# One load queue in order of need, pre-scaled down weights for the last block, a last output tile in two halves, and new order priorities in a transformer block on one core

## The chip, the cores and the metric

The kernel runs on one core of one Trainium2 chip. The metric is the device time of one execution in microseconds (us). "Span" is the time from the first to the last instruction in a profile; the timed figure is about 1.8 us longer (span 222.2, time 224.05 for the profiled run of the kernel before).

Each run carries the mean clock that was granted to the matmul engine: 1.0 is full speed. A run is called slow when it takes over 1.5% more than the fastest of the same kernel. Comparisons below are between fast runs, unless a sentence says otherwise.

## The reference

A transformer block on x of 2048 tokens by 448 features, in bf16. A condition vector c of 448 numbers gives six vectors of 448.

```python
mod = (silu(c) @ w_mod).reshape(1, 6, 1, 448)
sa, ca, ga, sb, cb, gb = [mod[:, i] for i in range(6)]
h = layernorm(x) * (1 + ca) + sa
x = x + ga * attention(h, wqkv, wo)   # 16 heads of 28; each token sees 8 tokens, at distances 0, 2, ..., 14
h = layernorm(x) * (1 + cb) + sb
gate, up = h @ W_gate, h @ W_up       # 448 -> 1792
x = x + gb * ((gate * (gate > 0) * up) @ W_down)
```

## The kernel before

The kernel is a list of operations. Each has an engine, a cost in ns, a priority, and what it reads and writes. At build time a greedy scheduler (`_Plan`) takes these and fixes, once and for all, the order of instructions on each engine: PE (matmuls), ScalarE (ACT), VectorE (DVE), GpSimd (POOL) and SP (which issues loads). On the chip nothing is reordered; an engine whose next instruction isn't ready waits.

The two numbers SWITCH and XLAT and the table of priorities steer the scheduler. The kernel computes the same whatever they are.

```python
PR = {
    "ln1": [537, 334, 2613, 2241],
    "qk": [711, 1230, 2349, 2507],
    # ... cut: ten more rows like these
    "misc": [2507, 2310, 2251, 237],
}
class _Plan:
    SWITCH = 105.0      # expected cost of a change of PE tiling shape
    XLAT = 95.0         # expected latency from one engine to another
    # ...
    # in schedule(): among the ready operations of an engine, the smallest priority number goes first
                sel = min((c for c in cl if c[0] <= tmin + slack[e]), key=lambda c: (c[1], c[2]))
```

Loads are put on SP's queue, except for two on ACT's:

```python
        load_x(0, 2, -9, eng=ACTE)                                        # x tiles 0 and 1, 224 KB
        load(crow[:], c..., ["crow"], 4096, -9, eng=ACTE)                 # c, 0.9 KB in 112 rows
        for i, (k0, k1) in enumerate(PARTS_A):
            load(wmod[0:112, k0:k1, 0:2 * D], ...)                        # first modulation's weights
            if i == 0:
                load_x(2, 4, -8)
        # ... cut: Wv, Wqk, x 4-8, the attention gate's weights, x 8-12, wo
        load_x(12, 16, -4)
        load(wmod[0:112, :, 3 * D:6 * D], ..., ["wmodB0", "wmodB1"], ...) # second modulation's weights, 1176 KB
        # ... cut: Wgate, Wup, Wdown
```

The head of the kernel needs two things before it can transform the first tokens: silu(c), by exp on ACT, then add, reciprocal and multiply on DVE, then the modulation matmuls on PE; and the layer-norm statistics of the tokens, by `bn_stats` on DVE. When both are there, PE transposes the normalized tokens and ACT and DVE write them back as `hT` with scale and shift. Then come the first matmuls of size, the value projection.

The output stage and the last down projection:

```python
        def stage_out(t, buf, eng, eprio):
            o = _Buf(o_slots)
            op(DVE, 620, ... tensor_tensor(o.at, buf.at[:, 0:D], gbc[:, 1, :], ALU.mult) ...)   # times gb, from PSUM
            op(eng, 400 if eng == DVE else 1030, ... tensor_tensor(o.at, o.at, x_sb[:, t, :], ALU.add) ...)
            op(SP, 0, ... dma_start(out2d[128 * t:128 * t + 128, :], o.at) ...)

        def stage_down1(b, hh, prio, eprio):       # blocks 0 and 3; blocks 1 and 2 use 64-row pairs
            for j in range(4):
                # ... 14 matmuls of 128x448 into buf
                stage_out(4 * b + j, buf, DVE if b == NB - 1 else POOL, eprio)
```

The softmax here doesn't subtract the row's maximum and nothing guards it: scores larger than these inputs give would overflow.

## Time and profile before

| | before |
|---|---|
| time, median of 3 runs | 224.74 us (224.7 to 225.2) |
| span, granted clock | 222.2 us, 1.000 |
| PE busy | 212.7 us (96%) |
| first value matmul | 11.58 us |
| last down stage (56 matmuls) starts | 207.09 us |

These are lines of the page of the kernel before: busy time by engine, the busy share in 40 equal slices in tenths (5.6 us each), and the granted clock.

```profile
PE 212.7 (96%) x2452; PEld 102.7 (46%) x2452; DVE 143.3 (65%) x299; ACT 119.5 (54%) x210; POOL 49.1 (22%) x73
...
PE   7699999989999999999999999999999999999992
...
DVE  2889999888879967842387659569444304544251
ACT  2658799989879697340286676822333301433200
...
PEclk9999999999999999999999999999999999999999
...
PE 87%; DVE 4%; ACT 3%; DMA 3%; issue 1%
```

PE is the bottleneck: it is 87% of the chain that ended last (the bottom line). It isn't the bottleneck everywhere. In the first two slices it is not full, and from slice 4 to 13 DVE and ACT are each busy 70% or more, so that a delay of theirs can become a wait of PE's. The clock is full throughout.

PE's waits between 10 and 75 us, in the kernel before (columns: engine, output and line that waited, what it waited for: us in total, times, longest):

```profile
PE psF L832 <- DVE qT L818: 0.5, 1, 0.5
PE psF L619 <- DVE hb L556: 0.5, 1, 0.5
PE psF L619 <- DVE hT L696: 0.4, 1, 0.4
PE psF L681 <- ACT kT L703: 0.2, 1, 0.2
```

These are few: between 11.58 and 72 us PE is busy for 58.59 of 60.42 us.

The head, in the timeline of the kernel before. Columns: start, duration, engine, source line, operation, output<-input, count; in brackets the idle time before it and what ended that.

```profile
0.77 0.45 ACTq L446 DMA_DIRECT2D x_sb<-in_A_x_dram  x1
1.25 0.49 ACTq L446 DMA_DIRECT2D crow<-in_c_dram  x1
...
5.49 0.63 DVE L538 BATCH_NORM_STATS2 st<-x_sb 128x6 f32<-128x448 bf16 x1 [2.80 <-DMA x_sb<-in_A_x_dram]
...
6.93 0.21 ACT L490 ACTIVATE cexp<-crow 112x4 f32<-112x4 bf16 x1 [4.91 <-DMA crow<-in_c_dram]
...
7.85 0.55 PE L507 MATMUL psF<-silu,bigR 112*128 112x1 bf16 x16 [1.71 <-DVE silu L493]
```

DVE waits for the first activations until 5.49, ACT for c until 6.93. The chain of waits shows the later of the two, as "1.25 5.66 DMA crow<-in_c_dram".

The tail, in the timeline of the kernel before:

```profile
207.09 10.77 PE L930 MATMUL psF<-Wd,bigR 128*128 128x448 bf16 x56
...
217.89 0.62 DVE L891 TENSOR_TENSOR o_sb<-psF,gbc 128x448 bf16<-128x448 f32 x1 [1.53 <-PE psF L930]
218.55 0.39 DVE L893 TENSOR_TENSOR o_sb<-o_sb,x_sb 128x448 bf16<-128x448 bf16 x1
```

After the last matmul come a multiply from PSUM and an add, about 1.1 us, before the last store can be issued. All of it is on the critical path.

### The profile page before, as it was taken

The numbers are of one execution on the slowest core, as the hardware profiler recorded it, in microseconds if no ns is written. First come the engines' busy times: TensorE is split into PE (matmuls) and PEld (weight loads), VectorE is DVE, ScalarE is ACT, GpSimd is POOL, SyncE is SP. The second block draws the span as 40 slices with busy tenths as digits, with TensorE's granted clock in tenths as the row PEclk, the third lists the DMA queues.
The fourth block names the chain that finished last, engine by engine and source line by source line (L and its number), as shares of the span: only waits on it lengthen the run. The fifth ranks groups of instructions, "written<-read, shape, count | busy, mean of one in ns | idle before, by whom it ended". The sixth has DMA issues, their size and how long they took to land.

```text
span 222.2 us, 5740 instructions
## 1 busy us (share of the span) xinstructions
PE 212.7 (96%) x2452; PEld 102.7 (46%) x2452; DVE 143.3 (65%) x299; ACT 119.5 (54%) x210; POOL 49.1 (22%) x73
## 2 busy tenths in 40 slices
PE   7699999989999999999999999999999999999992
PEld 3344345555534445445544455554444454444450
DVE  2889999888879967842387659569444304544251
ACT  2658799989879697340286676822333301433200
POOL 7402450310220020028302001281660005100000
PEclk9999999999999999999999999999999999999999
DMA  6999999900130030021302000240440001100011
GB/s 174 334 274 237 200 229 238 274 5 3 27 71 3 0 52 3 0 52 41 103 24 47 3 3 1 50 96 31 91 109 21 3 0 41 44 0 3 1 41 43
DMA packets 19634, 16.52 MB, mean 74 GB/s; under 512 B 9624, under 2 KB 17880, under 8 KB 19608
## 3 DMA queue, kind: packets, MB, share of 16 engines
q1 hardware_dynamic: 19208, 15.92, 29.6%
q8 instruction: 19, 0.31, 0.6%
q10 hardware_dynamic: 400, 0.23, 0.4%
q14 instruction: 7, 0.06, 0.1%
HBM read 10.84 MB, written 1.84 MB: 57 GB/s over the span
## 4 chain that ended last, share of the span: by engine, by line
PE 87%; DVE 4%; ACT 3%; DMA 3%; issue 1%
PE psF L875 29%; PE psF L681 10%; PE psF L930 10%; PE psF L912 10%; PE psF L877 9%; PE psF L724 6%; PE psF L832 6%; PE psL L763 3%; DMA crow<-in_c_dram 3%; PE psF L796 2%; PE psF L808 1%; PE psF L619 1%; ACT EA L776 1%; DVE qT L696 1%; DVE EA L782 1%
## 5 line engine op out<-in xcount | busy, mean ns | idle before, releaser
L877 PE MATMUL psF<-h2T,Wgu 64*128 64x512 bf16 x392 | 87.7, 376 | 0.0
L875 PE MATMUL psF<-h2T,Wgu 64*128 64x512 bf16 x392 | 87.7, 376 | 0.0
L883 ACT ACTIVATE g_sb<-psF 128x512 bf16<-128x512 f32 x56 | 33.4, 597 | 52.8 <-PE psF L877 52.5
L885 DVE TENSOR_TENSOR bigR<-psF,g_sb 128x512 bf16<-128x512 f32 x56 | 38.6, 690 | 30.4 <-ACT g_sb L883 30.2
L875 PEld LDWEIGHTS psF<-h2T,Wgu 64*128 64x128 bf16 x392 | 36.2, 94 | 33.8 <-DVE st L538 0.2
L877 PEld LDWEIGHTS psF<-h2T,Wgu 64*128 64x128 bf16 x392 | 36.2, 94 | 9.8
L776 ACT ACTIVATE EA<-psL 128x912 bf16<-128x912 f32 (+1 forms) x36 | 33.3, 925 | 12.6 <-PE psL L763 12.5
L556 POOL TENSOR_SCALAR hb<-x_sb,rstd,nmr 128x448 bf16<-128x448 bf16 x22 | 15.5, 716 | 87.2 <-DVE nmr L549 81.5
L681 PE MATMUL psF<-hT,Wqk 64*128 64x512 bf16 x224 | 27.9, 377 | 0.5 <-ACT kT L703 0.2
L782 DVE TENSOR_TENSOR EA<-EA,maskA 128x912 bf16<-128x912 bf16 (+1 forms) x36 | 23.1, 646 | 6.6 <-ACT EA L776 6.1
L891 DVE TENSOR_TENSOR o_sb<-psF,gbc 128x448 bf16<-128x448 f32 x16 | 9.7, 622 | 22.7 <-PE psF L930 13.2
L912 PE MATMUL psF<-Wd,bigR 64*128 64x448 bf16 x224 | 22.5, 349 | 0.0
L538 DVE BATCH_NORM_STATS2 st<-x_sb 128x6 f32<-128x448 bf16 x32 | 19.7, 614 | 3.1 <-DMA x_sb<-in_A_x_dram 2.8
L930 PE MATMUL psF<-Wd,bigR 128*128 128x448 bf16 x112 | 21.5, 353 | 0.0
L893 POOL TENSOR_TENSOR o_sb<-o_sb,x_sb 128x448 bf16<-128x448 bf16 x12 | 12.2, 1031 | 26.3 <-DVE o_sb L891 26.3
L681 PEld LDWEIGHTS psF<-hT,Wqk 64*128 64x128 bf16 x224 | 9.6, 94 | 13.3 <-PE psF L681 2.8
L930 PEld LDWEIGHTS psF<-Wd,bigR 128*128 128x128 bf16 x112 | 10.8, 98 | 10.4 <-issue 0.4
L912 PEld LDWEIGHTS psF<-Wd,bigR 64*128 64x128 bf16 x224 | 10.8, 94 | 9.9
L832 PE MATMUL psF<-wo_pad,qT 64*128 64x448 bf16 x128 | 14.6, 350 | 0.6 <-DVE qT L818 0.5
L724 PE MATMUL psF<-Wv,hT 64*128 64x448 bf16 x126 | 14.2, 352 | 0.3
L572 POOL TENSOR_SCALAR h2T<-h2T,modc 128x512 bf16<-128x512 bf16 (+1 forms) x14 | 11.0, 797 | 13.4 <-DMA h2T<-hb 13.4
L818 DVE TENSOR_TENSOR qT<-psF,lnD 128x456 bf16<-128x456 f32 (+1 forms) x18 | 11.3, 627 | 2.2 <-ACT lnD L816 2.1
(75 smaller groups left out, 212.9 us busy)
## 6 DMA issues: line engine op xcount, KB each, us to landing
out_dram<-o_sb SPq DMA_DIRECT2D x16, 112.0 KB, 1.7
Wd<-in_B_W_down_dram SPq DMA_DIRECT2D x1, 1568.0 KB, 26.5
x_sb<-in_A_x_dram SPq DMA_DIRECT2D x3, 448.0 KB, 9.3
Wgu<-in_B_W_gate_dram SPq DMA_DIRECT2D x3, 448.0 KB, 17.5
Wgu<-in_B_W_up_dram SPq DMA_DIRECT2D x3, 448.0 KB, 19.5
bigR<-in_w_mod_dram SPq DMA_DIRECT2D x1, 1176.0 KB, 15.5
bigR<-in_w_mod_dram SPq DMA_DIRECT2D x2, 392.0 KB, 6.7
h2T<-h2T SPq DMA_DIRECT2D x3, 256.0 KB, 3.1
```

Source lines behind the costliest of these rows:

```text
L538: op(DVE, 613, lambda e: e.bn_stats(stt[:, t, :], x_sb[:, t, :]), r=[("x", t)] + list(extra), w=[(tag, "st", t)], prio=prio)
L681: last = e.matmul(bufs[sec].at, Wqk[h0:h0 + 64, k, c0:c0 + 128], hT[h0:h0 + 64, k, KOFF + TB * b:KOFF + TB * b + TB], start=(phase == 0 an ...
L724: last = e.matmul(bufs[i].at[0:nk, 0:D], hT[h0:h0 + 64, k, KOFF + k0:KOFF + k0 + nk], Wv[h0:h0 + 64, k, :], start=(phase == 0 and n == 0), ...
L776: return e.activation(dst, src, ACT.Exp)
L782: return e.tensor_tensor(d, d, msk[0:nk, None, 0:nq].to_broadcast([nk, 8, nq]), ALU.mult)
L832: last = e.matmul(bufs[i].at[:, 0:D], qT[h0:h0 + 64, g, s0:s0 + 128], wo_pad[h0:h0 + 64, g, :], start=(phase == 0 and g == 0), stop=(phase ...
L875: e.matmul(bufs[0].at, Wgu[0:64, c, 128 * f:128 * f + 128], h2.at[0:64, kg, :], start=(c == 0), stop=(c == 6))
L877: last = e.matmul(bufs[1].at, Wgu[64:128, c, 128 * f:128 * f + 128], h2.at[64:128, ku, :], start=(c == 0), stop=(c == 6))
L883: op(ACTE, _act(TB), lambda e, gs=gs, gb=bufs[0]: e.activation(gs.at, gb.at, ACT.Relu), r=[bufs[0]], w=[gs], prio=eprio)
L885: op(DVE, _dve(TB), lambda e, gs=gs, ub=bufs[1], f=f: e.tensor_tensor(hh.at[:, f, :], ub.at, gs.at, ALU.mult), r=[bufs[1], gs] + ([hh] if ...
L912: last = e.matmul(bufs[i].at[:, 0:D], hh.at[rows[i], f, 128 * (j + i):128 * (j + i) + 128], Wd[rows[i], f, :], start=(phase == 0 and f == ...
L930: last = e.matmul(buf.at[:, 0:D], hh.at[:, f, 128 * j:128 * j + 128], Wd[:, f, :], start=(f == 0), stop=(f == NF - 1))
```

## The change

The intent, part by part:

1. **Queue.** c goes first and alone on ACT's queue; the first activations go first on SP's queue, ahead of the modulation weights. All large loads are then in one queue, in the order in which they are needed.
2. **Tail.** Under the last gate/up stage GpSimd multiplies the down weights by gb once (14 multiplies). The last block then needs one add from PSUM instead of a multiply and an add, and its last tile is computed and added in two halves of 224 columns, so that the final add is shorter.
3. **Order.** A new table of priorities and new cost parameters for the scheduler: another order on every engine.

```diff
 PR = {
-    "ln1": [537, 334, 2613, 2241],
-    "qk": [711, 1230, 2349, 2507],
+    "ln1": [1460, 60, 2830, 2572],
+    "qk": [191, 2415, 509, 2324],
     # ... cut: every other row of the table changes likewise
 }
-    SWITCH = 105.0
-    XLAT = 95.0
+    SWITCH = 95.0
+    XLAT = 80.0
+    OVERLAP = {PE: 0.0, ACTE: 85.0, DVE: 75.0, POOL: 40.0, SP: 0.0}
 # ... cut: the scheduler lets an operation start OVERLAP ns before the end of the one ahead on its engine;
 # ... cut: three cost estimates (_mm, PE_DRAIN, transposes) are lowered
-        load_x(0, 2, -9, eng=ACTE)
         load(crow[:], c.rearrange("o (p k) -> (o p) k", k=4), ["crow"], 4096, -9, eng=ACTE)
+        load_x(0, 2, -9)
 # ... in stage_down1
-                stage_out(t, buf, DVE if b == NB - 1 else POOL, eprio)
+                scaled = b == NB - 1
+                cols = ((0, D // 2), (D // 2, D)) if scaled and j == 3 else ((0, D),)
+                for n, (n0, n1) in enumerate(cols):
+                    # ... the 14 matmuls, on columns n0 to n1
+                    if scaled:
+                        op(DVE, _dve(n1 - n0), ... tensor_tensor(
+                            o.at[:, n0:n1], buf.at[:, 0:n1 - n0], x_sb[:, t, n0:n1], ALU.add) ...)
+                # ... then one store of the tile
 # ... in the loop over blocks, before the last gate/up stage
+            if b == NB - 1:
+                for f in range(NF):
+                    op(POOL, 1030, lambda e, f=f: e.tensor_tensor(Wd[:, f, :], Wd[:, f, :], gbc[:, 1, :], ALU.mult),
+                       r=[("Wd", f), ("gbc", 1)], w=[("Wd", f)], prio=3000, port=True)
```

## The prediction

> **What bounds it now.** The tensor engine (PE). The page shows PE busy 96% at full clock, and the chain of waits is 87% PE. Busy time hides stalls, so I took starts from the timeline: a gate/up group of 14 matmuls starts 1.51 us before the next, the last 56 down matmuls take 10.7 us. From the first real matmul (11.58 us) to the last (217.9) are 206.3 us; summing matmuls at those undisturbed pitches leaves about 190. The other 16 us, by my count: 66 changes of tiling shape at about 0.11 us (7 us), two modulation groups (1 us), and 5 to 6 us of real waits, nearly all before 72 us, where the timeline shows gaps and the windows show VectorE and ScalarE about 90% busy. After 72 us PE is nearly gapless. Outside PE: an 11.6 us head and a 4.3 us tail.
>
> **Removed, added, moved.**
> - Head: today the 0.9 KB load of c waits behind an activation load on its queue; issued 1.25, landed 6.91. Then exp, silu and the second layer-norm statistics run late. With c first I estimate landing near 3 us (an output store lands in 1.7 us), and the first activations earlier as they no longer share with modulation weights. The bytes do not change; the Trainium skill ("Trainium Kernel Development and Optimization", Key Constraints) says queues share the same 16 DMA engines, and the trace agrees (DMA saturated, slices 2 to 8). First value-projection matmul: 10.5 instead of 11.58, gain 1.1 us.
> - But the new order puts all 32 modulation matmuls of the second layer norm early on PE (before the first softmax-denominator matmul), and they wait for a load that lands at 27.1 us today and has as many bytes ahead of it after. By content PE arrives near 25: a stall of 1 to 2 us that gives the head's gain back. Before, these matmuls ran at 33.6.
> - Tail: one add from PSUM (0.62 us) replaces multiply (0.62) plus add (0.39), and for the last tile covers 224 columns, about 0.39. Last matmul to store shrinks from 1.08 to about 0.45; 14 more matmuls cost about 0.06. Net 0.6 us, wholly on the critical path.
> - Gating: 14 GpSimd multiplies, about 1.03 us each as in the output add (14.4 us), plus two output adds, must fit under the last gate/up stage (21.2 us). They do, with about 4 us to spare: no cost, no gain but the tail's.
> - Order: the same matmuls and 64 shape changes instead of 66 (0.2 us). The Trainium skill ("TensorEngine Tiling (Array Packing)", Key Properties) says a mode change drains PE; the trace shows 0.11 us. The new priorities can recover only part of the 5 to 6 us of waits; I guess 1 to 2 us net.
>
> **Predicted time: 222.4 us**, 8 in 10 between 220.3 and 224.2. Chances: faster by over 2% 0.10, within 2% 0.87, slower 0.03.
>
> **What would show it.** Right: c landing before 4 us; first value matmul near 10.5; a PE wait on the modulation-weight DMA near 25 to 27; PE's last stage 21.2 us and then 10.8 without a wait on GpSimd; last matmul to last store about 0.45 us; matmul content unchanged; PE gaps before 72 us summing to 4 to 5 us. Wrong: the modulation matmuls finding their weights landed, or PE waiting for GpSimd at the last down stage.
>
> **What would make it wrong.** If those weights land by 25, or VectorE and ScalarE run ahead during the stall so that later gaps vanish, the gain reaches 4 us or more. If the new order starves PE between 28 and 72 us (both helpers near saturation there), nothing is won. GpSimd multiplies slowed by VectorE traffic to over 1.3 us each would delay the last stage.

## The result, and the profile after

| | before | after |
|---|---|---|
| time, median of 4 runs | 224.78 us (224.70 to 225.20) | 222.00 us (221.39 to 226.04) |
| ratio of fast runs | | 0.9864 (95%: 0.9833 to 0.9895) |

A ratio is the mean time of one kernel's fast runs over that of the other's of the same rounds, so it isn't quite the ratio of the medians. The 1.4% is real.

Of the four runs after, three took 221.39 to 222.34 us at a clock of 0.997 to 0.999, and one, which is the profiled one, took 226.04 at 0.983: a slow run. Its profile shows how a slow run goes and is used for that. For the fast picture I use the profile of an experiment, split_load, whose order on the compute engines is the changed kernel's and which differs only in that one load is cut in two. It ran as fast (221.66 us by median) and its profiled run was fast: span 219.3 us at clock 0.999.

The head of that fast run, in the timeline of split_load:

```profile
0.74 0.47 SPq L478 DMA_DIRECT2D x_sb<-in_A_x_dram  x1
0.77 0.42 ACTq L478 DMA_DIRECT2D crow<-in_c_dram  x1
...
3.04 0.21 ACT L523 ACTIVATE cexp<-crow 112x4 f32<-112x4 bf16 x1 [1.02 <-DMA crow<-in_c_dram]
...
4.19 1.15 DVE L571 BATCH_NORM_STATS2 st<-x_sb 128x6 f32<-128x448 bf16 x2
...
6.03 0.54 PE L540 MATMUL psF<-silu,bigR 112*128 112x1 bf16 x16
```

exp of c starts at 3.04 instead of 6.93, the statistics at 4.19 instead of 5.49, the modulation matmuls at 6.03 instead of 7.85. The first value matmul starts at 10.32 instead of 11.58.

The tail of the same run:

```profile
204.77 10.80 PE L968 MATMUL psF<-Wd,bigR 128*128 128x448 bf16 x70
...
214.27 0.39 DVE L974 TENSOR_TENSOR o_sb<-psF,x_sb 128x224 bf16<-128x224 f32 x1 [0.72 <-PE psF L968]
215.61 0.39 DVE L974 TENSOR_TENSOR o_sb<-psF,x_sb 128x224 bf16<-128x224 f32 x1 [0.95 <-PE psF L968]
```

After the last matmul stands one add of 0.39 us. From the start of this stage to the end of the span are 14.53 us (219.3 minus 204.77), before 15.11 (222.2 minus 207.09): the tail is about 0.6 us shorter. GpSimd's 14 multiplies took about 14 us and ended at 199.65, 5.1 us before the stage that reads them, in this run as in the slow one.

PE's waits between 10 and 75 us, to set beside those of the kernel before. The fast run, split_load:

```profile
PE psF L757 <- ACT hT L674: 1.4, 2, 1.2
PE psF L829 <- DVE EA L815: 0.4, 1, 0.4
```

The slow run of the changed kernel:

```profile
PE psF L725 <- DVE mv L541: 2.4, 1, 2.4
PE psF L508 <- DMA bigR<-in_w_mod_dram: 0.7, 1, 0.7
PE psF L797 <- DVE EA L783: 0.4, 1, 0.4
```

In the slow run PE waits twice as long at the same place, for DVE instead of ACT, and then also for the second modulation's weights. What DVE was doing stands in its timeline, in the same slow run:

```profile
22.94 0.63 DVE L539 BATCH_NORM_STATS2 st<-x_sb 128x6 f32<-128x448 bf16 x1 [1.49 <-DMA x_sb<-in_A_x_dram]
23.49 0.98 DVE L643 TENSOR_SCALAR hT<-psF,modc 128x512 bf16<-128x512 bf16 x2
```

The statistics of tile 12 stand ahead of the `hT` write-back in DVE's order, and their load is late. PE waits for the write-back, which ends at 24.47 us (the list of waits names `mv`, a short instruction of DVE that ends at about the same time). In the slow run 15 of the load's 16 parts had landed by 20.1 us and the last at 22.9; in the fast run all 16 had by 19.8. The Trainium skill ("DMA: Bandwidth & Descriptors", Why a DMA increments its semaphore by 16 and not by 1) says that the 16 engines finish independently and that only the full count means all data has landed. This agrees: one late part of 16 held everything up by 2.8 us. Why one part is late in some runs isn't shown.

Then comes the larger loss. These are windows of the slow run, chosen 3.41 us long. Columns: window, length, busy time (and instructions) of PE, weight loads, DVE, ACT and POOL, then the granted clock, DMA share and GB/s.

```profile
21.85:25.26 3.41, 0.97 (x17) 0.52 (x16) 2.32 (x6) 2.27 (x3) 2.86 (x3) 1.00 1.05 192
25.26:28.67 3.41, 3.41 (x26) 1.20 (x22) 2.88 (x10) 1.86 (x4) 0.00 (x0) 0.50 1.05 213
28.67:32.08 3.41, 2.67 (x69) 1.73 (x68) 1.23 (x7) 1.67 (x4) 2.81 (x4) 1.00 1.05 228
32.08:35.49 3.41, 3.41 (x20) 1.23 (x21) 2.63 (x5) 2.11 (x4) 1.42 (x2) 0.50 1.01 223
```

The granted clock is half for two windows of 3.41 us, each after a window in which PE was partly idle. The Trainium skill ("TensorE: Matmul & The Clock Gate", Part 1: The HAM clock gate) says that the clock goes to 4/8 after at least one idle window of about 3.4 us, and that these windows run freely. The trace agrees in the size of the window and in the half, but not in the idleness: PE was busy for 0.97 and 2.67 us of the two windows before (more in the last section). Each such window costs up to 1.7 us, half its length, so the two cost up to 3.4. With the 1.2 us of longer waiting for `hT` (2.44 against 1.24) and the 0.74 us on the weights that is about 5.4 us as an upper bound, and the spans differ by 4.9.

### The profile page after: what moved, and what is told of

Read it like the earlier page. It is cut to its first block, busy times and chain, and to the rows that moved or that the text cites. A ratio compares the mean times of both kernels' runs of the same rounds, so it can differ in the third digit from the quotient of the medians.

```text
span 224.2 us, 5763 instructions
## 1 busy us (share of the span) xinstructions
PE 215.1 (96%) x2466; PEld 105.5 (47%) x2466; DVE 140.4 (63%) x297; ACT 115.3 (51%) x208; POOL 63.5 (28%) x88
## 4 chain that ended last, share of the span: by engine, by line
PE 85%; DMA 8%; POOL 3%; SPq 1%; DVE 1%; issue 1%; POOLq 0%
PE psF L876 35%; PE psF L936 10%; PE psF L913 9%; PE psF L682 9%; DMA bigR<-in_w_mod_dram 8%; PE psF L833 6%; PE psL L764 4%; PE psF L725 3%; PE psF L878 3%; PE psF L797 3%; PE psF L809 2%; SPq L447 1%; POOL maskA L423 1%; PE psF L529 1%; POOL wo_pad L418 1%
## 5 line engine op out<-in xcount | busy, mean ns | idle before, releaser
L557 POOL TENSOR_SCALAR hb<-x_sb,rstd,nmr 128x448 bf16<-128x448 bf16 x23 | 16.4, 719 | 77.3 <-DVE nmr L550 59.4
L682 PE MATMUL psF<-hT,Wqk 64*128 64x512 bf16 x224 | 27.4, 384 | 0.0
L783 DVE TENSOR_TENSOR EA<-EA,maskA 128x912 bf16<-128x912 bf16 (+1 forms) x36 | 22.5, 630 | 4.3 <-ACT EA L777 4.1
L936 PE MATMUL psF<-Wd,bigR 128*128 128x448 bf16 (+1 forms) x126 | 21.6, 332 | 0.0
L539 DVE BATCH_NORM_STATS2 st<-x_sb 128x6 f32<-128x448 bf16 x32 | 18.8, 610 | 1.5 <-DMA x_sb<-in_A_x_dram 1.5
L725 PE MATMUL psF<-Wv,hT 64*128 64x448 bf16 x126 | 15.6, 378 | 2.7 <-DVE mv L541 2.4
L892 DVE TENSOR_TENSOR o_sb<-psF,gbc 128x448 bf16<-128x448 f32 x12 | 7.2, 622 | 15.9 <-PE psF L936 7.0
L936 PEld LDWEIGHTS psF<-Wd,bigR 128*128 128x128 bf16 x126 | 12.1, 98 | 9.3 <-issue 0.4
L992 POOL TENSOR_TENSOR Wd<-Wd,gbc 128x448 bf16<-128x448 bf16 x14 | 13.9, 1033 | 0.0
## 6 DMA issues: line engine op xcount, KB each, us to landing
bigR<-in_w_mod_dram SPq DMA_DIRECT2D x1, 1176.0 KB, 17.7
```

The source lines that it names most:

```text
L539: op(DVE, 613, lambda e: e.bn_stats(stt[:, t, :], x_sb[:, t, :]), r=[("x", t)] + list(extra), w=[(tag, "st", t)], prio=prio)
L682: last = e.matmul(bufs[sec].at, Wqk[h0:h0 + 64, k, c0:c0 + 128], hT[h0:h0 + 64, k, KOFF + TB * b:KOFF + TB * b + TB], start=(phase == 0 an ...
L725: last = e.matmul(bufs[i].at[0:nk, 0:D], hT[h0:h0 + 64, k, KOFF + k0:KOFF + k0 + nk], Wv[h0:h0 + 64, k, :], start=(phase == 0 and n == 0), ...
L783: return e.tensor_tensor(d, d, msk[0:nk, None, 0:nq].to_broadcast([nk, 8, nq]), ALU.mult)
L936: last = e.matmul(buf.at[:, 0:n1 - n0], hh.at[:, f, 128 * j:128 * j + 128], Wd[:, f, n0:n1], start=(f == 0), stop=(f == NF - 1))
```

## The experiments

All are on the chip, and the kernel before ran beside them (medians 224.76, 224.89 and 224.81 us in the three batches; the first batch has after_again, only_queue, only_tail and only_order, the third early_tr, c_first, dose_after and dose_queue_tail, the second the other four). The three batches ran on three different chips, so that across batches the ratios to the kernel before are the better comparison. Every result was correct.

The scheduler decides the order, so an edit to one load would reshuffle all engines. So I let the scheduler run once, kept the order of every engine, applied the edit to that order, and computed buffers and semaphores anew from it ("order kept"). Only after_again has no edit, and in only_tail and queue_tail the scheduler, with the old priorities and costs, placed the tail's new operations itself.

The expectations of the first batch took as theory that the head's gain is mostly taken back by waits (only_queue) and that most of the gain comes from the order (only_order). The rivals were that the head's gain carries through to the end, and that the order alone does nothing or loses. Both theories failed; the rivals came nearer.

### after_again: the changed kernel once more

No edit. It fixes the size of the gain and of the spread.

> The changed kernel once more, with five timed rounds, to see its spread and, if it comes so, a profile in the fast state. My theory: its spread is wider than that of the kernel before (224.7 to 225.2) because its tensor engine waits for two loads between 20 and 30 us, and a late load both adds its delay and lets the granted clock fall. Expected: median 221.5 to 222.5, spread over 0.5 us, fast ratio 0.983 to 0.990; in the profile the first value matmul at 10.3 us and a wait of the second modulation's matmuls for their weights. Rival (the state is chance and has nothing to do with the loads): slow runs would show no longer wait for a load than fast ones.

Measured: 221.68 us by median, runs 226.77 (slow, clock 0.983), 222.09, 221.50, 221.35 and 221.68; ratio 0.9858 (0.9829 to 0.9888). The gain repeats. The wider spread that was expected does not show: the fast runs span 0.7 us, those of the kernel before 1.9 us in the same batch (224.16 to 226.10). The slow run repeats too, again the first of its set and again with one of the 16 parts of a load late and two half-clock windows. In every set of an experiment the first run is also the profiled one, so whether being first or being profiled matters is open.

### only_queue: the new queue with the old order

```diff
-        load_x(0, 2, -9, eng=ACTE)
         load(crow[:], ..., eng=ACTE)
+        load_x(0, 2, -9)                # order of all engines otherwise kept as before
```

> The kernel before with its instruction order kept on every engine, and only the load of c first on its queue and the first activations first on the other. Theory (the head's gain is real, 1.1 us, but is taken back by waits for loads and by VectorE near saturation until 72 us): between 0.2 and 0.7 us faster than before. Rival (the head's gain carries through to the end, since the tensor engine is the bottleneck all along): 1.0 to 1.2 us faster.

Measured: 223.16 us (222.50 to 223.54), ratio 0.9924 (0.9897 to 0.9952): a gain of 1.6 us by medians (1.2 us between the profiled spans), more than the theory (0.2 to 0.7) and the rival (1.0 to 1.2) had said. These are lines of its timeline:

```profile
3.24 0.20 ACT L524 ACTIVATE cexp<-crow 112x4 f32<-112x4 bf16 x1 [1.22 <-DMA crow<-in_c_dram]
3.91 0.63 DVE L572 BATCH_NORM_STATS2 st<-x_sb 128x6 f32<-128x448 bf16 x1 [1.22 <-DMA x_sb<-in_A_x_dram]
...
10.06 3.30 PE L758 MATMUL psF<-Wv,hT 64*128 64x448 bf16 x28
```

The first value matmul comes 1.52 us earlier than before (11.58), and the last down stage 1.20 us earlier (205.89 against 207.09). So most of the head's gain lasts to the end. The later loads also come earlier in this profile: tiles 12 to 15 at 19.3 us instead of 20.4 and the second modulation's weights at 25.6 instead of 27.1. That need not be the queue's doing: over the seven profiled runs with this stream of loads uncut, the weights land anywhere from 24.8 to 29.6 us.

### only_tail: the pre-scaled weights and the split tile with the old order and queue

```diff
+            if b == NB - 1:
+                for f in range(NF):
+                    op(POOL, 1030, ... Wd[:, f, :] *= gbc[:, 1, :] ...)
 # ... and stage_down1 as in the change; priorities, costs and loads as before
```

> The kernel before with its order kept, and only the pre-gated down weights and the split last tile. Theory (all of it is on the critical path): 0.6 us faster, 0.4 to 0.7; last matmul to the last store's issue falls from 1.1 to about 0.5 us; the last down stage does not wait for GpSimd. Rival (the gating slows something, or the split costs array time): no gain or a loss.

Measured: 224.40 us by median; the five fast runs lie between 224.09 and 224.47; ratio 0.9977 (0.9951 to 1.0002). That is 0.4 us by medians, with an interval that touches zero. Its profiled run took 316.15 us at a clock of 0.661. No other run did anything like it, and I have no explanation, so I use no profile of this kernel.

### only_order: the new order with the old queue and the old tail

```diff
 # ... the changed kernel with the old stage_down1 and no pre-scaled weights; order kept, then
+        x0 = T[("x", 0)]                # the load of x tiles 0 and 1
+        order[SP].remove(x0)
+        order[ACTE].insert(0, x0)       # back to ACT's queue, ahead of c
```

> The changed kernel's new order on every engine, with the old two load queues and the old last stage. Theory (most of the gain of 3 us comes from the order, by fewer waits before 72 us): 1.5 to 2.5 us faster than before. Rival (the gain comes from the head and the tail, and the order alone does nothing or loses by its early modulation matmuls): between 0.5 us faster and 1 us slower.

Measured: 226.13 us (224.97 to 226.67), ratio 1.0051 (1.0022 to 1.0079), clock 0.990 to 0.992 in five of six runs: the new order alone is a loss. Its timeline shows why:

```profile
7.33 0.17 DVE L526 TENSOR_SCALAR cexp<-cexp 112x4 f32<-112x4 f32 x1 [4.64 <-ACT cexp L525]
...
7.83 1.15 DVE L573 BATCH_NORM_STATS2 st<-x_sb 128x6 f32<-128x448 bf16 x2
...
10.80 0.40 PE L654 MATMUL psF<-ident,hb 128*128 128x128 bf16 x4 [1.65 <-ACT hb L593]
```

The new order has DVE handle c ahead of the first statistics. With the new queue c is there first and that is right. With the old queue c lands at 7.1 us, and DVE sits idle for 4.64 us although the activations had landed at 5.6. PE then has a hole of 1.65 us. The windows of the same run by 1 us show what follows:

```profile
12.00:13.00 1.00, 0.55 (x6) 0.49 (x6) 1.00 (x6) 0.95 (x2) 0.00 (x0) 0.81 1.14 259
13.00:14.00 1.00, 1.00 (x7) 0.47 (x5) 0.15 (x2) 0.77 (x3) 0.00 (x0) 0.50 1.11 259
14.00:15.00 1.00, 1.00 (x7) 0.29 (x8) 1.00 (x5) 1.00 (x3) 0.00 (x0) 0.50 1.09 312
15.00:16.00 1.00, 0.94 (x6) 0.14 (x2) 0.23 (x2) 0.43 (x1) 0.00 (x0) 0.50 1.14 243
```

One window of half clock, of about 3.4 us. The new order fits the new queue; neither is to be judged without the other.

### queue_tail: queue and tail with the old order

```diff
 # ... the kernel before with the tail of the change, its order kept, then x tiles 0 and 1 first on SP's queue
+        order[ACTE].remove(x0)
+        order[SP].insert(0, x0)
```

> Everything of the change but the new order: the kernel before's order on every engine, the new load queue, the new last stage. If the parts of the gain simply add (queue 1.6 us, tail 0.4 to 0.5 us by the runs so far), it is 2.0 to 2.2 us faster than before, near 222.6, and the order is worth what is left to the changed kernel, about 1 us. If the order has no worth of its own, this is as fast as the changed kernel (3.1 us faster than before). It should show no slow first run from loads, as its second modulation's matmuls come 8 us later.

Measured: 222.12 us (221.87 to 222.28, four runs, clock 0.998 to 1.000), ratio 0.9863 (0.9826 to 0.9900). This is the main result: with the old order, queue and tail reach 0.9863, and the whole change 0.9858 to 0.9864. The new table of priorities adds between nothing and half a microsecond, which these runs don't separate from zero. The 222.12 us are themselves half a microsecond less than the 222.6 expected if the two parts add; why isn't shown. In its profiled run, too, one part of a load was late (tiles 12 to 15 at 21.8 us, the weights at 27.4), and PE's clock stayed 1.00: the old order needs both later, the second modulation's matmuls at 33.65 us in the kernel before, against 26.00 in the new order.

### late_mod: the second modulation's matmuls moved later in the new order

```diff
+        for oid in [T[("mm", 8, 0)], T[("mm", 8, 1)], T[("gbc", 1)] - 1]:   # 32 matmuls and the gate row
+            self.move(order, PE, oid, T[("tr", 2, 3)])                     # to before block 2's transposes
+        # ... their reads on DVE and their memset moved likewise
```

> The changed kernel with only the second modulation's 32 matmuls, its gate row's 4 and their reads moved later, to just before the third block's transposes, where their weights have long landed; the rest of the order is kept. Theory (in the changed kernel the tensor engine stands about 1 us, from 24.7 to 25.7, for these weights in a fast run): 0.5 to 1.2 us faster than the changed kernel's 221.7. Rival (VectorE and ScalarE near saturation until 72 us set the pace, and the wait only moves): within 0.3 us of 221.7.

Measured: 223.95 us (223.92 to 224.20), ratio 0.9948. If PE had lost a wait for weights there, moving would have gained; it lost 2.3 us, which neither the theory nor the rival had foreseen. PE's waits in this run, between 10 and 75 us:

```profile
PE psF L761 <- ACT hT L678: 1.3, 2, 1.1
PE psL L800 <- ACT EA L813: 1.2, 1, 1.2
PE psF L833 <- DVE EA L819: 1.0, 2, 0.6
PE psF L845 <- ACT kT L740: 0.5, 1, 0.5
PE psF L869 <- DVE hT L679: 0.3, 1, 0.3
```

A new wait of 1.2 us on ACT's exponentials stands where the matmuls had been. The next group of logits starts at 29.20 us here and at 29.30 in split_load, where the modulation matmuls run before it. So this stretch is paced by ACT, and the matmuls had filled time in which PE had nothing else to do. Put later, they take PE's time where PE is the bottleneck; in split_load the 32 matmuls take 0.95 us and the gate row's 4 take 0.93. The rest of the 2.3 us isn't accounted for.

### late_both: late_mod, and the statistics of tile 12 moved behind the write-back

```diff
+        order[DVE].remove(T[(1, "st", 12)])
+        order[DVE].insert(order[DVE].index(T[("hT", 1, 3, 0)]) + 1, T[(1, "st", 12)])
```

> As late_mod, and VectorE's statistics of the first of the last four tiles moved behind its two writes of the second block's transposed activations, so that these no longer stand behind the landing of the last activations. Theory: in fast runs as late_mod (those activations land at 19.3, before VectorE comes to them near 21); in a run with a late load (a slow first run, as the changed kernel had twice) about 2 us faster than it, and a granted clock above 0.995 instead of 0.983.

Measured: 224.88 us (224.45 to 225.88), ratio 0.9993: another 0.9 us lost, and no gain over the kernel before is left. Moving the statistics was meant to free the write-back from a late load. In this run PE's wait on ACT's `hT` stayed at 1.1 us, and the wait on DVE's masks grew from 1.0 to 1.5 us in total. No profiled run of it had a late load, so what was expected for such a run wasn't tested. Both edits were failures as improvements.

### split_load: the second modulation's weights in two loads

```diff
-        load(wmod[0:112, :, 3 * D:6 * D], ..., ["wmodB0", "wmodB1"], ...)
+        load(wmod[0:112, :, 3 * D:5 * D + 64], ..., ["wmodB0", "wmodB1"], ...)   # what the 32 matmuls read
+        load(wmod[0:112, :, 5 * D + 64:6 * D], ..., ["wmodG1"], ...)             # the rest, for the gate row
```

> The changed kernel with its order kept and only the second modulation's load cut in two, so that the weights of shift and scale (5/7 of it) land about 1.8 us sooner, near 23.8, before the tensor engine comes to them at 24.7. Theory: the wait of about 1 us is gone and 0.5 to 1 us comes off 221.7; the gate row's weights are still in time. Rival, as for late_mod: within 0.3 us.

Measured: 221.66 us by median (221.08 to 223.74; five of six between 221.08 and 221.80), ratio 0.9859 (0.9816 to 0.9903): no different from the changed kernel. PE's timeline around the place:

```profile
23.40 0.93 PE L757 MATMUL psF<-Wv,hT 64*128 64x448 bf16 x8 [1.24 <-ACT hT L674]
24.26 0.37 PE L796 MATMUL psL<-qT,kT 28*128 28x114 bf16 x8
24.57 1.50 PE L757 MATMUL psF<-Wv,hT 64*128 64x448 bf16 x14
26.00 0.95 PE L540 MATMUL psF<-silu,bigR 112*128 112x1 bf16 x32
```

The weights landed at 22.9 us and PE came for them at 26.00 without a wait. In only_queue, which has the same stream of loads uncut, they landed at 25.6, also before 26.00. So a run without a late part need not stall on this load, cut or not. No fast run of the changed kernel itself was profiled, and early_tr below, a fast run with a late part, did wait 0.3 us. But landing at 22.9 us gained nothing over the changed kernel (221.66 against 221.68 us in after_again), which speaks against a stall in its fast runs that costs 1 to 2 us.

### early_tr: block 1's transposes earlier

```diff
+        # PE: T[("tr", 1, 3)] ahead of block 0's last query/key group
+        # ACT and DVE: the four hT write-backs of block 1 ahead of that group's write-backs
```

> A candidate for a better version. In the fast profile of split_load the tensor engine stands 1.4 us (21.8 to 23.4) after the second block's transposes, until VectorE and ScalarE have written them back. Here the transposes come before the last query/key group instead of after it, so that this group's matmuls run during the write-back, as in the order of before; everything else is the changed kernel's. If that wait is on the critical path: 0.4 to 1.0 us faster than the changed kernel's 221.7. If ScalarE paces this stage (the first softmax exp cannot start sooner), within 0.3 us of it. The runs of late_mod and late_both speak for the latter.

Measured: 223.09 us (221.88 to 225.07), ratio 0.9926. It was an attempt to remove the remaining 1.2 us wait on `hT`. That wait shrank to 0.2, and PE waited in front of the logits instead (1.8 us in three entries). No gain, rather a loss of about 1.4 us, which neither expectation had. The profiled run was fast, at full clock, though one part of its loads was late: tiles 12 to 15 landed at 21.6 us and the weights at 26.9, and PE waited 0.3 us for these. So a late part doesn't always bring the clock down.

### c_first: c ahead of the activations, on the old queue, with the old order

```diff
+        self.move(order, ACTE, T["crow"], T[("x", 0)])   # on ACT's queue: c, then x tiles 0 and 1
```

> The kernel before with its order kept, and only the two loads of the second queue swapped: c first, then the first activations, still on that queue. It tells what in the new queue is worth 1.6 us (only_queue). If it is c's place alone: 1.3 us or more faster than before, c landing near 3.2 us and the first value matmul near 10.1. If the activations must leave the second queue too (they compete there with the modulation weights, and all loads ran earlier with one queue: the last-needed one landed at 25.6 instead of 27.1): 0.3 to 1.0 us, and the second modulation's weights land near 27.

Measured: 225.69 us by median, ratio 1.0045 (1.0003 to 1.0087), in two groups: three runs at 225.03 to 225.07 with a clock of 0.996 to 1.000, three at 226.30 to 227.86 with 0.985 to 0.988. Even the better group gains nothing, where 0.3 us or more was expected either way. The profiled run is of the worse group; in it c landed at 4.3 us instead of 6.9, yet:

```profile
6.13 0.63 DVE L569 BATCH_NORM_STATS2 st<-x_sb 128x6 f32<-128x448 bf16 x1 [3.43 <-DMA x_sb<-in_A_x_dram]
...
7.62 0.14 DVE L522 TENSOR_SCALAR cexp<-cexp 112x4 f32<-112x4 f32 x1
```

The old order has DVE do the first statistics before it touches c, and the activations landed at 6.1 us, later than before (5.5). So c's place in the queue alone does not make the head shorter; the first activations have to move too: first on SP's queue they land at 3.45 to 3.89 us, on ACT's queue beside the modulation weights at 5.5. Whether moving them alone would do wasn't tested. The Trainium skill ("Trainium Kernel Development and Optimization", Key Constraints) says that the queues share 16 DMA engines and interleave, so that another queue saves only issue time; this agrees, as in the kernel before the first load of each queue, issued at 0.74 and 0.77, landed at 5.2 and 5.5 us. The slow group's profile has half clock from 10.8 to 17.7 us, two windows long.

### dose_after and dose_queue_tail: a useless load of 573 KB ahead of tiles 12 to 15

```diff
+        load(Wd[:, 0:5, :], B_W_down[0:640, :]..., [("dose", 0)], 1, -4, issue=1.0)
         load_x(12, 16, -4)
```

The same edit to the changed kernel (dose_after) and to queue_tail (dose_queue_tail). It makes late loads on purpose. (The profile counts in 1024 bytes and shows this load as 560 KB.)

> The changed kernel with 573 KB more to load (data that nobody reads) just before the last activations, so that these and the second modulation's weights land about 2.2 us later, near 21.6 and 27.8. If the new order is what makes the changed kernel sensitive to late loads: 1.5 to 4 us slower than 221.7, and the granted clock falls under 0.997. If its slow runs are chance that has nothing to do with loads: under 0.5 us slower.

> The same 573 KB in the kernel with the old order, the new queue and the new last stage (222.1 us). Its second modulation's matmuls stand near 32 us, after the load has landed even so: under 0.5 us slower than 222.1, granted clock 0.997 or more.

Measured: dose_after 223.18 us, in two groups, 222.47 to 222.82 at clock 1.00 and 223.55 to 223.88 at 0.990 to 0.992; ratio 0.9923 (0.9893 to 0.9954). dose_queue_tail 223.31 us (222.34 to 223.70), all at 0.997 or above; ratio 0.9925 (0.9893 to 0.9956). PE's waits in dose_after, between 10 and 45 us (a third one, of 0.4 us, is left out):

```profile
PE psF L757 <- DVE mv L573: 1.5, 1, 1.5
PE psF L540 <- DMA bigR<-in_w_mod_dram: 1.1, 1, 1.1
```

With the load at 27.5 us the new order does wait for it, as in the slow runs. But my theory, that only the new order suffers, falls: the old order lost 1.2 us too, where I had expected little. Its profiled run was one of its faster ones and shows only 0.4 us of one new wait, so where it loses is open. Nor is it the landing of these two loads: they came at 21.4 and 27.1 us, and in queue_tail's profile without the dose at 21.8 and 27.4. What may remain particular to the new order under late loads is the lowered clock: three of the six dosed runs of the new order have a mean clock of 0.990 to 0.992, and the one of them that was profiled has 0.87 between 30 and 42 us; no dosed run of the old order is below 0.997. With six runs each that is a hint: the kernel before, with its old order and no dose, is itself at 0.987 to 0.992 in three of its 33 runs beside the experiments.

## Why the prediction was right or wrong

The time was right: 222.4 predicted, 222.0 measured. The sum behind it was not.

- **What bounds it.** PE, rightly. But the "5 to 6 us of real waits" that the new order was to recover from are not in the trace: PE is idle for 1.83 us between 11.58 and 72 us before, and for 1.97 us between 10.32 and 72 us in the fast run of the new order. (Stalls inside what counts as busy don't show.) The changes of tiling shape were counted at 0.11 us each; the trace gives about 0.09 (last section).
- **Head, 1.1 us.** The size was about right: c at 3.0 to 3.2 us, the first value matmul at 10.32 (1.26 us earlier), with the old order 10.06. The mechanism was half right. I named c's place behind another load first and the activations second; c_first shows that c alone gives nothing with the old order.
- **"PE arrives near 25: a stall of 1 to 2 us that gives the head's gain back."** This is the step that failed. In the fast run PE comes at 26.00, after a wait of 1.24 us for a write-back, and finds the weights landed. Where they land later it does wait, but for less than predicted or in slower runs: 0.3 us in early_tr, 0.7 in the slow run, 1.1 in dose_after. And the wait doesn't take the head's gain: weights that land at 22.9 us (split_load) give no more than the changed kernel has, and in the fast profile the 1.26 us gained at the first value matmul are still there at the end. With the old order, where no such wait was predicted, the gain stays too: 1.6 us in only_queue.
- **Order, 1 to 2 us net.** Too much. Given the queue and the tail it is worth 0 to 0.5 us (222.12 against 221.68 to 222.00), and with the old queue it costs 1.4 us. The two errors, a stall that isn't paid and an order that earns less, cancelled: the total was right by luck.
- **Tail, 0.6 us.** Right: about 0.6 us from the profiles of split_load and queue_tail; 0.4 by medians in only_tail, with an interval that touches zero. The final add took 0.39 us as estimated.
- **Gating.** Right: about 1.03 us a multiply, hidden, with 5.1 us to spare (about 4 predicted).
- **Not foreseen.** The half-clock windows. I counted waits of 1 to 2 us as 1 to 2 us; a wait at the wrong time costs up to 1.7 us more for each window that follows.

In one sum, by profiles: of the 2.9 us between the spans 222.2 and 219.3, 1.26 are gone at the first value matmul, about 0.6 in the tail, and about 1.1 between the two. The last term belongs to the fastest run of split_load; by medians it is half as large or less. Where in the middle it comes from I didn't find: three hand edits to the order there each lost time, so the waits that one sees don't tell what the order is worth.

No version tried beats the changed kernel. queue_tail comes within half a microsecond and had no slow run in four, against two in nine of the changed kernel; four runs are too few to prefer it.

## What to carry to other kernels

When the chain of waits names one late load, look for a second wait beside it before costing the fix; here moving the load that was named gained nothing by itself. Put what is needed first at the front of one queue, and judge a static order only together with the arrival times it was made for, since an order that is right for one sequence of loads lost 0.5% with another. Count a hole in the matmul stream at more than its length when the clock can follow it down, and look at the clock in every run before explaining a few microseconds.

## What the Trainium skill lacked or had wrong

- "TensorE: Matmul & The Clock Gate", Part 1, gives an idle window of about 3.4 us as what brings the clock down, and its closing table asks for no idle gaps over about 3 us. The length and the half agree (0.50 over 25.26 to 28.67 and again over 32.08 to 35.49 us), but less idleness was enough: the longest gap before a dip was 2.44 us in the slow run and 1.65 in only_order, and in the windows before the dips PE was busy for 0.97 and 2.67 (slow run), 1.37 (only_order), 2.29 (dose_after) and 2.47 of 3.41 us (c_first). The busy share alone doesn't decide either: no dip followed a window with 1.92 us busy in after_again and one with 2.08 in late_mod. Elsewhere the page does speak of short idle times that bring the clock down and of transposes that don't count as busy in the same way; how much is enough it doesn't say.
- "Trainium Kernel Development and Optimization", Key Constraints, says that a second queue only saves issue time. It gives no figure for what an early load can lose by sharing: a 224 KB load issued at 0.77 us on ACT's queue, beside the other queue's loads, landed at 5.5 us; issued at 0.74 at the head of the one queue it landed at 3.45 to 3.89.
- No page that I read gives a figure for what a load of many tiny rows costs the loads around it. c is 0.9 KB in 112 rows; with it ahead of the first activations the second modulation's weights landed at 23.9 us (c_first), with it behind them at 27.1 (the kernel before) and 27.2 (only_order), with the same bytes in the same two queues. One run each, and in other kernels runs of one stream of loads differ by as much, so this may be chance.
- "DMA: Bandwidth & Descriptors" says that the 16 parts of a load finish independently, and gives no size for the spread. Here the last part of 448 KB came 0.4 us behind the fifteenth in a fast run (19.4 and 19.8) and 2.8 us in a slow one (20.1 and 22.9); but 2.5 us in a fast run of queue_tail too.
- "TensorEngine Tiling (Array Packing)", Key Properties, says that a change of tiling shape drains the array, and gives no cost. In the trace of the kernel before it is about 0.09 us: where the shape changes, the next matmul starts 0.31 us after one of 512 columns instead of 0.22, and 0.28 after one of 448 columns instead of 0.19.
